# Linear attention on one core: the stores of heads 28 and 29 become one set, shared between GpSimd and SP

## The chip, the core and the metric

The kernel runs on one core of a Trainium2 chip. The metric is device time in microseconds. The time before is the median of three runs, 167.97 us (167.58 to 168.05). The profile is of one more execution, which took 167.82 us; its span, from the first to the last instruction, is 166.5 us. Times inside the kernel are given in us from the start of that span.

A few words for a new reader. TensorE (PE) does matrix products, VectorE (DVE), ScalarE (ACT) and GpSimd (POOL) do elementwise work, and SyncE (SP) issues most of the transfers. A transfer is cut up among 16 DMA engines, and each of them adds one to the transfer's semaphore when its own share has landed.

## The reference: what is computed

Inputs q, k, v are bf16 of shape (1, 32, 2048, 128): 32 heads of 2048 rows of 128. For each head:

```
phi_q = where(q > 0, q + 1, exp(q)) + 1e-6
phi_k = where(k > 0, k + 1, exp(k)) + 1e-6
kv    = phi_k^T v              # 128 x 128
z     = sum over rows of phi_k # 128
out   = (phi_q kv) / (phi_q z + 1e-6)
```

Each head reads 3 x 512 KB and writes 512 KB, so the kernel moves 50.33 MB in and 16.78 MB out.

## The kernel before

**Tiling.** A head's 2048 rows lie on 128 partitions, 16 rows to a partition: partition p holds rows 16p to 16p+15, so a partition's share of a head is 16 x 128 x 2 bytes = 4 KB, in one piece in DRAM and in one piece in SBUF. In what follows "a row" of a store means one partition's share, as in the change's title. `NBI` = 6 input buffers each for k, q and v; `NBO` = 10 output buffers `o_sb`, so head h uses output buffer h % 10: heads 28 and 29 lie in the neighbouring buffers 8 and 9, and heads 30 and 31 in 0 and 1.

**Stages of a head.** ACT takes exp(k) (line 368); GpSimd takes the relu of k (372) and adds part of the two halves of phi_k (390); DVE clips the exponential (382); PE builds kv and z in PSUM (413, 320), and ACT copies them to SBUF (430). PE transposes q (436), ACT and DVE make its two halves (447, 454, 456, 468), PE multiplies them with kv (483, 484). DVE adds 1e-6 to the denominators (506), takes reciprocals (512) and multiplies into `o_sb` (517, 524). For the last two heads ACT does a part of these multiplications (536).

**Order.** A planner holds all operations. Every one has an engine and a number, its key; on each engine the operations are emitted in the order of the keys, and the planner adds the semaphore waits that the data need. Loads and stores are emitted on SP. The store of head h has the key h + 1 + 0.18 h (line 575), which places stores behind the loads of later heads, more so the later the head. Behind the last load, SP's list holds only stores; each waits for the last DVE multiplication of its head. The last operation of GpSimd's list is the memset of ones for head 31 (line 426); after it GpSimd has nothing to do.

**The stores at the end** (lines 570 to 584). A store is issued by `store`, which takes a range of partitions. All heads up to 30 are stored by one transfer of 128 rows, except head 29: `PARTS` cuts it into transfers of 51, 13 and 64 rows, all three on SP and on the semaphore of output buffer 9. Head 31 is stored by two transfers of 128 partitions: nine tiles (288 KB), then seven (224 KB). At the very end SP waits for the semaphores of all output buffers.

Of the kernel before, what the change touches and what calls it, by code (L numbers as in the profile page):

```python
# [7 lines left out]
P = 128  # L8
# [223 lines left out]
def bass_standalone__linear_attn_elu__prompt_kernel(  # L232
# [8 lines left out]
    NT = 16  # L241
# [3 lines left out]
    NBI = 6  # L245
    NBO = 10
# [2 lines left out]
    NG = 7  # L249
    HALF = NT * P // 2  # L250
    LAST = NH - 1
    PARTS = {LAST - 2: (51, 13, 64)}

    ADD = (10, 11, 12, 13, 14)
    EVEN, ODD = tuple(range(0, NT, 2)), tuple(range(1, NT, 2))
# [7 lines left out]
    of = out.rearrange("b h s d -> (b h) s d")  # L263

    with ExitStack() as es:
        def sb(name, shape, dt):
            return es.enter_context(nc.sbuf_tensor(name, shape, dt))
# [13 lines left out]
        o_sb = sb("o_sb", [P, NBO, NT, D], bf16)  # L281
# [12 lines left out]
        def dma_sem(name):  # L294
            return dsems[name]

        for n, c in (("k", NBI), ("q", NBI), ("v", NBI), ("va", 1), ("o", NBO + 1)):
            for i in range(c):
                dsems[(n, i)] = es.enter_context(nc.semaphore(f"s_{n}{i}"))

        pl = Plan()

        def rows(x, h):
            return x[h].rearrange("(p j) d -> p (j d)", j=NT)
# [11 lines left out]
               reads=[("id0",)], writes=[("ident",)])  # L316
# [34 lines left out]
        for h in range(NH):  # L351
# [3 lines left out]
            bi, b2, b3, bo = h % NBI, h % 2, h % 3, h % NBO  # L355

            def load(name, buf, src, key, h=h, bi=bi):
                dst, rws = buf[:, bi], rows(src, h)
                if name == "v":
# [9 lines left out]
                   reads=[("k", bi)], writes=[("ek", b2)])  # L369
# [8 lines left out]
            else:  # L378
# [4 lines left out]
                   reads=[("ek", b2)], writes=[("emk", b3)], kind="emk")  # L383
# [36 lines left out]
            if h:  # L420
                pl.add("pe", at("kv", -1.2), lambda pe, kv=kv, t=both_of: kv(pe, t, start=True),
                       reads=[("emk", b3), ("rk", b3, 0), ("rk", b3, 1)] + base, writes=[("bankkv",)])
            pl.add("pe", at("kv", -1.199), lambda pe, kv=kv, t=one_of, f=h == 0: kv(pe, t, start=f, stop=f),
                   reads=[("phix" if h == 1 else "phik", b3)] + base + ([] if h else [("first",)]), writes=[("bankkv",)])
            if h:
                pl.add("pool", h + 0.6, lambda g, bi=bi: g.memset(_ap(vfull, bi * VW + GAP + D - 1, [[2 * D, NT // 2], [1, 1]]), 1.0),
                       reads=[("v", bi)], writes=[("vo", bi)], kind="vo")
                pl.add("pe", at("kv2", -0.2985), lambda pe, kv=kv: kv(pe, ODD, stop=True),
                       reads=[("phik", b3), ("emk", b3), ("rk", b3, 0), ("rk", b3, 1), ("v", bi), ("vo", bi)], writes=[("bankkv",)])
            pl.add("act", at("kvs", -0.95), lambda a, b3=b3: a.activation(kvs_sb[:, b3, :], kvz_ps[:, 0:NC], ACT.Copy),  # L430
                   reads=[("bankkv",)], writes=[("kvs", b3)], kind="kvs")
# [31 lines left out]
            else:  # L463
# [5 lines left out]
                   reads=[("eq", b2, 0), ("eq", b2, 1)], writes=[("emq", b3)], kind="emq")  # L469
# [100 lines left out]
            def store(t0, t1, key, parts, slot, p0=0, p1=P, h=h, bo=bo):  # L570
                pl.add("sp", key, lambda sp: sp.dma_start(rows(of, h)[p0:p1, t0 * D:t1 * D],
                                                          o_sb[p0:p1, bo, t0:t1].rearrange("p j d -> p (j d)")),
                       reads=[("o", bo, p) for p in parts], dma=("o", slot))

            late = h + 1.0 + 0.18 * h
            if h < LAST:
                p0 = 0
                for n in PARTS.get(h, (P,)):
                    store(0, NT, late, ("t", 0, 1, 2, 3, 4), bo, p0, p0 + n)
                    p0 += n  # L580
                assert p0 == P
            else:
                store(0, 9, late, (0, 1, 2), bo)
                store(9, NT, late + 0.01, (3, 4, "t"), NBO)

# [29 lines left out]
```

## Time and profile before

| what | value |
|---|---|
| median of 3 runs | 167.97 us |
| the profiled execution | 167.82 us |
| its span | 166.5 us |
| PE, DVE, ACT, GpSimd busy | 156.0, 152.3, 155.0, 106.3 us |
| bytes moved, mean rate over the span | 67.25 MB, 404 GB/s |
| last load issued by SP (v of head 31) | 135.79 us |
| GpSimd's last instruction | 156.37 us, 0.13 us long |
| store of head 28 issued | 152.48 us |
| the three stores of head 29 issued | 157.20 to 158.48 us |
| store of head 30 issued | 160.94 us |
| the two stores of head 31 issued | 162.20 and 162.87 us |

How to read it: the busy times are of the whole span, so they say little of the last ten microseconds, in which the engines stop one after the other and only transfers are left. Those are read from the table of windows (busy time of each engine, share of the DMA engines' time in which a packet was under way, and GB/s) and from the semaphore increments that the trace records, one for each DMA engine that has landed its share of a transfer.

### The profile page before, as it was taken

The numbers are of one execution on the slowest core, as the hardware profiler recorded it, in microseconds if no ns is written. First come the engines' busy times: TensorE is split into PE (matmuls) and PEld (weight loads), VectorE is DVE, ScalarE is ACT, GpSimd is POOL, SyncE is SP. The second block draws the span as 40 slices with busy tenths as digits, with TensorE's granted clock in tenths as the row PEclk, the third lists the DMA queues.
The fourth block names the chain that finished last, engine by engine and source line by source line (L and its number), as shares of the span: only waits on it lengthen the run. The fifth ranks groups of instructions, "written<-read, shape, count | busy, mean of one in ns | idle before, by whom it ended". The sixth has DMA issues, their size and how long they took to land.

```text
span 166.5 us, 6269 instructions
## 1 busy us (share of the span) xinstructions
PE 156.0 (94%) x2819; PEld 145.3 (87%) x2453; DVE 152.3 (91%) x270; ACT 155.0 (93%) x143; POOL 106.3 (64%) x128
## 2 busy tenths in 40 slices
PE   7789999999999999999999999999999999999960
PEld 0259999999999999899999989999998999999950
DVE  0587999999999999999999999999999999999991
ACT  3979999999999999999999999999999999998790
POOL 2405788676767877676778867676787767677300
PEclk9999999999999999999999999999999999999998
DMA  5999999999999999999999999999999999999986
GB/s 205 345 417 421 413 415 419 412 407 418 417 416 419 422 417 417 422 421 411 424 420 414 423 421 415 419 421 415 422 420 416 422 421 418 418 421 418 415 310 239
DMA packets 18605, 67.25 MB, mean 404 GB/s; under 512 B 2082, under 2 KB 2210, under 8 KB 18594
## 3 DMA queue, kind: packets, MB, share of 16 engines
q1 hardware_dynamic: 18592, 67.12, 99.4%
q8 instruction: 5, 0.08, 0.2%
q14 instruction: 6, 0.05, 0.1%
q10 hardware_dynamic: 2, 0.00, 0.0%
HBM read 50.33 MB, written 16.78 MB: 403 GB/s over the span
## 4 chain that ended last, share of the span: by engine, by line
DVE 58%; PE 17%; POOL 12%; ACT 6%; issue 3%; DMA 2%; DVEq 0%
DVE o_sb L524 20%; POOL rk_sb L390 12%; DVE rq_sb L456 11%; DVE emk_sb L382 10%; DVE emq_sb L468 9%; PE kvz_ps L413 6%; PE o_ps L483 5%; PE o_ps L484 5%; ACT ek_sb L368 3%; DVE rden_sb L512 3%; DVE o_sb L517 3%; ACT eq_sb L447 2%; DMA k_sb<-in_k_dram 2%; DVE den_sb L506 2%; DVE rk_sb L390 1%
## 5 line engine op out<-in xcount | busy, mean ns | idle before, releaser
L413 PE MATMUL kvz_ps<-v_sb,rk_sb 128*128 128x129 bf16 (+1 forms) x512 | 67.0, 220 | 2.8 <-DVE rk_sb L390 1.0
L524 DVE TENSOR_TENSOR o_sb<-o_ps,rden_sb 128x768 bf16<-128x768 f32 (+2 forms) x62 | 67.8, 1135 | 0.0
L390 POOL TENSOR_TENSOR rk_sb<-rk_sb,emk_sb 128x640 bf16<-128x640 bf16 x30 | 41.9, 1395 | 39.5 <-DVE emq_sb L468 38.2
L372 POOL TENSOR_SCALAR rk_sb<-k_sb 128x1024 bf16<-128x1024 bf16 (+1 forms) x60 | 64.1, 1068 | 2.5 <-DMA k_sb<-in_k_dram 2.5
L483 PE MATMUL o_ps<-kvs_sb,emq_sb 128*128 128x129 bf16 (+1 forms) x536 | 65.2, 217 | 0.0
L484 PE MATMUL o_ps<-kvs_sb,rq_sb 128*128 128x129 bf16 (+1 forms) x536 | 64.4, 217 | 0.0
L368 ACT ACTIVATE ek_sb<-k_sb 128x2048 bf16<-128x2048 bf16 x32 | 61.0, 1907 | 2.6 <-DMA k_sb<-in_k_dram 2.6
L447 ACT ACTIVATE eq_sb<-xT_ps 128x2048 bf16<-128x2048 bf16 (+1 forms) x33 | 60.0, 1821 | 2.0 <-PE xT_ps L436 2.0
L413 PE MATMUL kvz_ps<-v_sb,emk_sb 128*128 128x129 bf16 (+1 forms) x338 | 53.3, 221 | 0.6 <-DVE emk_sb L382 0.3
L413 PEld LDWEIGHTS kvz_ps<-v_sb,rk_sb 128*128 128x128 bf16 x512 | 46.1, 98 | 7.6 <-POOL rk_sb L390 2.7
L483 PEld LDWEIGHTS o_ps<-kvs_sb,emq_sb 128*128 128x128 bf16 x536 | 51.2, 98 | 0.8 <-issue 0.3
L484 PEld LDWEIGHTS o_ps<-kvs_sb,rq_sb 128*128 128x128 bf16 x536 | 51.3, 98 | 0.0
L436 PE MATMUL xT_ps<-ident,q_sb 128*128 128x128 bf16 x512 | 33.8, 219 | 0.6 <-DMA q_sb<-in_q_dram 0.4
L436 PEld LDWEIGHTS xT_ps<-ident,q_sb 128*128 128x128 bf16 x512 | 29.9, 98 | 5.1 <-DMA q_sb<-in_q_dram 4.2
L413 PEld LDWEIGHTS kvz_ps<-v_sb,emk_sb 128*128 128x128 bf16 x338 | 32.5, 98 | 0.9 <-DVE emk_sb L382 0.5
L320 PE MATMUL kvz_ps<-ones_sb,rk_sb 128*128 128x1 bf16 x232 | 31.3, 165 | 0.0
L454 ACT ACTIVATE rq_sb<-xT_ps 128x1024 bf16<-128x1024 bf16 x30 | 30.9, 1029 | 0.0
L382 DVE TENSOR_SCALAR emk_sb<-ek_sb 128x2048 bf16<-128x2048 bf16 x32 | 22.0, 688 | 5.6 <-ACT ek_sb L368 5.6
L456 DVE TENSOR_SCALAR rq_sb<-xT_ps 128x1024 bf16<-128x1024 bf16 x34 | 23.3, 690 | 1.1 <-PE o_ps L484 1.0
L468 DVE TENSOR_SCALAR emq_sb<-eq_sb 128x2048 bf16<-128x2048 bf16 x32 | 22.1, 690 | 0.0
L320 PE MATMUL kvz_ps<-ones_sb,emk_sb 128*128 128x1 bf16 x121 | 19.9, 166 | 0.0
L430 ACT ACTIVATE kvs_sb<-kvz_ps 128x129 bf16<-128x129 f32 x32 | 9.0, 281 | 1.6 <-PE kvz_ps L413 0.9
(28 smaller groups left out, 49.2 us busy)
## 6 DMA issues: line engine op xcount, KB each, us to landing
k_sb<-in_k_dram SPq DMA_DIRECT2D x32, 512.0 KB, 15.0
q_sb<-in_q_dram SPq DMA_DIRECT2D x32, 512.0 KB, 15.1
v_sb<-in_v_dram SPq DMA_DIRECT2D x32, 512.0 KB, 15.1
out_dram<-o_sb SPq DMA_DIRECT2D x30, 512.0 KB, 15.3
out_dram<-o_sb SPq DMA_DIRECT2D x1, 288.0 KB, 3.7
out_dram<-o_sb SPq DMA_DIRECT2D x1, 256.0 KB
out_dram<-o_sb SPq DMA_DIRECT2D x1, 224.0 KB, 3.6
out_dram<-o_sb SPq DMA_DIRECT2D x1, 204.0 KB
```

The costliest lines, as they stand in the source:

```text
L320: return pe.add_instruction(mybir.InstMatmult(start_tensor_calc=start, stop_tensor_calc=stop, ldweights=False, bass_skip_group_check=True, ...
L368: lambda a, bi=bi, b2=b2: a.activation(ek_sb[:, b2, :], k_sb[:, bi, :], ACT.Exp),
L372: pl.add(eng, key, lambda e: e.tensor_scalar(rk_sb[:, b3, c], k_sb[:, bi, c], BIG, 0.0, op0=ALU.min, op1=ALU.max), reads=[("k", bi)] + ([( ...
L382: lambda d, b2=b2, b3=b3: d.tensor_scalar(emk_sb[:, b3, :], ek_sb[:, b2, :], 1.0, EPS, op0=ALU.min, op1=ALU.add),
L390: return e.tensor_tensor(out=a, in0=a, in1=b, op=ALU.add)
L413: last = pe.matmul(kvz_ps[:, 1 - l:NC], lhsT=w, rhs=v_sb[:, bi, c - l:c + D], start=first, stop=fin, skip_group_check=True)
L436: last = pe.transpose(xT_ps[:, j * P:(j + 1) * P], q_sb[:, bi, j * P:(j + 1) * P], ident[:])
L447: halves[part] = pl.add("act", key, lambda a: a.activation(eq_sb[:, b2, c], xT_ps[:, c], ACT.Exp), reads=both[part:part + 1] or both, writ ...
L456: f = lambda d: d.tensor_scalar(rq_sb[:, b3, c], xT_ps[:, c], 0.0, None, op0=ALU.max)
L483: pe.matmul(o_ap, lhsT=emq_sb[:, b3, t * P:(t + 1) * P], rhs=kvs_sb[:, b3, c0:c1], start=True, stop=False)
L484: return pe.matmul(o_ap, lhsT=rq_sb[:, b3, t * P:(t + 1) * P], rhs=kvs_sb[:, b3, c0:c1], start=False, stop=True)
L524: pl.add("dve", key, lambda d: d.tensor_tensor(out=o_sb[:, bo, 3 * g0:3 * g1, :].rearrange("p (a b) d -> p a b d", b=3), in0=_ap(full, bas ...
```

## The change

Heads 28 and 29 are no longer stored one by one. Nothing is issued when head 28 is ready. When head 29 is ready too, eight transfers are issued, each of which takes the same partitions of both heads, so that a row is now 2 x 4 KB: GpSimd issues one of 5 rows (partitions 0 to 4) and one of 99 rows (5 to 103), and SP issues six of 4 rows (104 to 127). The two on GpSimd get semaphores of their own; the six on SP use that of output buffer 9. Their key is that of head 29's store before. Bytes and values are the same, and all other operations stay as they are.

```diff
-    PARTS = {LAST - 2: (51, 13, 64)}
+    TWO = (("pool", NBO + 1, 5), ("pool", NBO + 2, 99)) + (("sp", NBO - 1, 4),) * 6
...
-        for n, c in (("k", NBI), ("q", NBI), ("v", NBI), ("va", 1), ("o", NBO + 1)):
+        for n, c in (("k", NBI), ("q", NBI), ("v", NBI), ("va", 1), ("o", NBO + 3)):
...
             late = h + 1.0 + 0.18 * h
-            if h < LAST:
+            if h == LAST - 2:
                 p0 = 0
-                for n in PARTS.get(h, (P,)):
-                    store(0, NT, late, ("t", 0, 1, 2, 3, 4), bo, p0, p0 + n)
+                for eng, slot, n in TWO:
+                    p = slice(p0, p0 + n)
+                    pl.add(eng, late, lambda e, p=p, bo=bo: e.dma_start(
+                        of[LAST - 3:LAST - 1].rearrange("h (p j) d -> p h (j d)", j=NT)[p], o_sb[p, bo - 1:bo + 1].rearrange("p h j d -> p h (j d)")),
+                        reads=[("o", b, x) for b in (bo - 1, bo) for x in ("t", 0, 1, 2, 3, 4)], dma=("o", slot))
                     p0 += n
                 assert p0 == P
-            else:
+            elif h < LAST and h != LAST - 3:
+                store(0, NT, late, ("t", 0, 1, 2, 3, 4), bo)
+            elif h == LAST:
                 store(0, 9, late, (0, 1, 2), bo)
                 store(9, NT, late + 0.01, (3, 4, "t"), NBO)
```

## The prediction

> **What bounds the kernel now.** I read the page first for the whole run, then the windows of its end, then SP's and GpSimd's lists, then the semaphore increments of the last stores.
>
> The page, whole run:
>
> ```profile
> span 166.5 us, 6269 instructions
> ...
> PE 156.0 (94%) x2819; PEld 145.3 (87%) x2453; DVE 152.3 (91%) x270; ACT 155.0 (93%) x143; POOL 106.3 (64%) x128
> ...
> DMA  5999999999999999999999999999999999999986
> ...
> q1 hardware_dynamic: 18592, 67.12, 99.4%
> ...
> out_dram<-o_sb SPq DMA_DIRECT2D x30, 512.0 KB, 15.3
> ...
> out_dram<-o_sb SPq DMA_DIRECT2D x1, 224.0 KB, 3.6
> ```
>
> PE, DVE and ACT are all over 90% busy, and the DMA engines are full from the second slice to the 38th; a store in the middle lands 15.3 us after its issue, so it stands in a queue. The change touches none of that, only the end. The windows there (busy time of each engine, clock, DMA share, GB/s):
>
> ```profile
> 158.00:160.00 2.00, 1.91 (x37) 1.74 (x35) 1.89 (x6) 1.83 (x8) 0.00 (x0) 1.00 1.01 363
> 160.00:161.00 1.00, 1.00 (x20) 0.90 (x16) 0.93 (x5) 0.93 (x5) 0.00 (x0) 1.00 0.75 258
> 161.00:162.00 1.00, 0.08 (x2) 0.00 (x0) 0.97 (x4) 0.97 (x4) 0.00 (x0) 1.00 0.58 238
> 162.00:163.00 1.00, 0.00 (x0) 0.00 (x0) 0.84 (x3) 0.73 (x3) 0.00 (x0) 1.00 0.99 373
> 163.00:164.00 1.00, 0.00 (x0) 0.00 (x0) 0.00 (x0) 0.00 (x0) 0.00 (x0) 1.00 0.99 387
> 164.00:165.00 1.00, 0.00 (x0) 0.00 (x0) 0.00 (x0) 0.00 (x0) 0.00 (x0) 1.00 0.70 276
> ```
>
> Between 160 and 162 the DMA engines idle for 0.25 + 0.42 us on the mean, before the last two heads are ready; from 164 on some have finished and others not. So the end is a matter of which DMA engine has how much left. SP's list (start, us, count of issues):
>
> ```profile
> 152.48 0.33 SPq L571 DMA_DIRECT2D out_dram<-o_sb  x1
> ...
> 157.20 1.28 SPq L571 DMA_DIRECT2D out_dram<-o_sb  x3
> ...
> 160.94 0.37 SPq L571 DMA_DIRECT2D out_dram<-o_sb  x1
> ...
> 162.87 0.37 SPq L571 DMA_DIRECT2D out_dram<-o_sb  x1
> ```
>
> These are heads 28, 29, 30 and the second part of 31. The increments of their semaphores, one per DMA engine, say the rest. Head 27 (issued 147.73): the first engine lands at 157.81, the eighth at 158.19, the fifteenth at 160.45, the sixteenth at 161.77. Head 28: 159.06, 159.43, 161.69, and 163.08. One engine, the laggard, is 1.3 to 1.4 us behind the fifteenth, and needs 1.39 us for a head's eight rows of 4 KB where the others need 1.25: 0.174 and 0.156 us a row. Head 29's last increment is at 163.96, head 31's last at 166.48, which is the end; ten of the sixteen were done by 164.94. The laggard is 0.88 us from 163.08 to 163.96, five rows by 0.174: one of the 13-row transfer, four of the 64-row one, none of the 51-row one, whose shares have 17 rows. So an end without a laggard could be up to 166.48 - 164.94 = 1.54 us earlier, and each row more for the laggard costs 0.17 us. Two others of the sixteen land within 0.11 us of it at the end, so a gain is partly covered by them.
>
> **The change part by part.**
>
> *How the shares fall.* The 128-row stores leave sixteen increments, and head 29's three leave 3 + 13 + 16 = 32. So a transfer goes to the largest number of engines up to 16 that divides its rows. By that, 5 rows go to five engines, 99 to eleven with nine rows each, 4 to four. A row is now two pieces of 4 KB. For heads 28 and 29 together an engine of the eleven gets 18 pieces, an engine of SP's four gets 12, one of the five 2. Before it was 8 of head 28 and 4, 5 or 22 of head 29; the laggard had 13. No row shows which engines a GpSimd transfer takes.
>
> *Removed:* four issues on SP (0.33 at 152.48, and 1.28 for three). SP waited before each, so that is worth nothing by itself. Head 28's 512 KB come to the queues 4.7 us later (157.20 for 152.48). The first engine runs out of head 27 at 157.81 and the fifteenth at 160.45. Head 30's store shows how soon new work starts: issue 160.94, first landing 163.47, 2.53 us, of which 8 x 0.156 = 1.25 are its rows; 1.28 is the start and the receipt. SP's first rows so start by 158.5. The leading engines idle about 0.7 us there; they idle before the last heads anyway (shares 0.75 and 0.58). Cost: nothing, as long as they have their pieces done by about 162.2, where head 30's start (160.94 + 1.28).
>
> *Added on SP:* six issues. The nearest row is the mean of the three at 157.20, 1.28 / 3 = 0.43; bounds 0.33 and 0.55. The sum is 2.6 us (2.0 to 3.3), to 159.8 (160.5 at most). Queued behind is head 30's store, at 160.94. Hidden; if head 30 were ready earlier, it would cost up to the 2.6 us. The four engines have 12 pieces x 0.156 = 1.9 us, done by about 160.7. But in 160 to 161 the rate was 258 GB/s at a share of 0.75, that is 344 at full share, for 413 to 422 between 150 and 158: the pieces of the part transfers took longer, single ones 300 to 440 ns in place of 159. At 440 the twelve last 5.3 us, to 163.8, and with 2.52 for heads 30 and 31 (163.96 to 166.48) end at 166.3. I take twice 0.156: no cost.
>
> *Added on GpSimd:* two issues behind its last instruction (156.37, 0.13 long); nothing is queued behind them there and no engine waits for GpSimd any more. The wait is for DVE's last multiplication of head 29, 157.17. Its cost is not in this trace. From below: SP's 0.33 each, pieces at 157.2 + 0.66 + 1.28 = 159.1. From above: GpSimd's longest row, 1.40, each, and 0.69 for one DVE operation in its way, 157.2 + 2.8 + 0.69 + 1.28 = 162.0. I take the middle, 160.5. Eighteen pieces are 2.81 us. On the fifteenth engine, free at 160.45, they end at 163.3 (164.8 by the upper bound), and with 2.52 at 165.8 (167.3).
>
> *The laggard* is not free until 161.77, so GpSimd's start costs it nothing. With 18 pieces, 3.13 us, it is done at 164.90 for 163.96 before: later by 0.94. At the others' rate it would be 2.81 and +0.62. Heads 30 and 31 follow on it as before.
>
> *The sum* for a laggard among the eleven: span 166.48 + 0.94 = 167.4, and with the 1.3 us around the span 168.8. That is against the profiled execution's 167.82, which is 0.15 below the median of 167.97; I leave the 0.15 to the range.
>
> [...]
>
> [...]
>
> **The rivals.**
>
> *A. The laggard is spared (faster).* It is none of the first three engines (five rows, above). If GpSimd's eleven leave it out, it has 2 pieces or none: done by 162.1, before head 30 starts. The fifteenth decides: 165.8, with 0.2 to 0.5 for slower pieces 166.0 to 166.3, and the time is 167.1 to 167.6; I say 167.3. For it: everything that ends after 164.94 is queueing. Against: eleven of sixteen hold any given engine with 0.69. It decides at thirteen pieces: below that the end moves earlier.
>
> *B. A middling share.* Fourteen pieces for the laggard (in SP's four with one of the five, or 99 rows cut into shares of seven): 161.77 + 14 x 0.174 = 164.21, later by 0.25, time 168.1; sixteen give 168.4.
>
> *C. GpSimd is late.* Non-laggards may start their 18 pieces until 163.96 - 2.81 = 161.15 without being later than the laggard was before, 3.95 us after the release at 157.20. Each us beyond costs one. At the upper bound, 162.0, the time is 168.7; at twice that issue cost, 165.5, some 172. For it: GpSimd has issued no transfer before in this kernel, a first one may be dear. Against: it is idle then.
>
> **How the numbers follow.** The laggard among the eleven 0.42, A 0.30 (5 of 16 is 0.31), B 0.13, C 0.15. About 0.3% (0.5 us) is what a measurement of this kernel can tell from no change: 167.5 to 168.5. A gives faster 0.27 and same 0.03; B same 0.08 and slower 0.05; the forecast same 0.02 and slower 0.40; C same 0.01 and slower 0.14. Together 0.27, 0.14, 0.59. The likeliest case alone spans 168.4 (rate 0.156) to 169.3 (0.5 more for slow pieces). The range goes down to A's 166.9 (the fifteenth undisturbed, and 0.2 less) and up to 169.9, where about half of C is left out.
>
> **What would show it.** Right: head 29's semaphores end at about 164.9 or later and one engine alone ends the kernel; head 30's issue stays near 160.9; the set leaves 5 + 11 + 24 increments, or sixteen per GpSimd transfer. A would show as all engines landing within about 1 us at the end. C would show as GpSimd's issues lasting over 1.4 us and a DMA share far below 1 between 158 and 161. The forecast is wrong if the laggard has few pieces, or if it is not slower in this execution.

## The result, and the profile after

The changed kernel takes 169.34 us (median of 10 runs, 168.14 to 170.35), the kernel before 167.91 us on the same chip (10 runs, 167.55 to 168.08). The ratio is 1.0084, 95% interval 1.0063 to 1.0105: it is slower by 0.8%. The sign and the range of the prediction held (168.8 us, 166.9 to 169.9). The reason that it gave did not. The profiled execution took 169.12 us. A few executions of the same kernel ran over 1.5% slower than its fastest; the ratios in this document leave them out, the medians and ranges do not.

The page of the changed kernel: the span, the DMA line of the forty slices, the two data queues (packets, MB, share of 16 engines) and the stores of the end (KB each, us from issue to landing).

```profile
span 167.8 us, 6274 instructions
...
DMA  5999999999999999999999999999999999999894
...
q1 hardware_dynamic: 18360, 66.27, 97.5%
q0 software_dynamic: 352, 0.85, 1.6%
...
out_dram<-o_sb POOLq DMA_DIRECT2D x1, 792.0 KB, 7.4
...
out_dram<-o_sb SPq DMA_DIRECT2D x1, 224.0 KB, 4.6
```

The span is 1.3 us longer than the 166.5 of before. Nothing before the last three slices has changed. GpSimd's 99 rows (792 KB) need 7.4 us from issue to landing, and the last store of the kernel, which was not touched, needs 4.6 in place of 3.6: it is held up by what stands ahead of it on some engine.

The end of the changed kernel by windows (busy time of PE, PEld, DVE, ACT, POOL; clock; DMA share; GB/s):

```profile
157.00:158.00 1.00, 1.00 (x22) 1.00 (x19) 0.93 (x5) 0.71 (x2) 0.94 (x2) 1.00 0.97 361
158.00:159.00 1.00, 0.91 (x17) 0.74 (x15) 0.96 (x3) 0.99 (x4) 0.72 (x1) 1.00 0.50 184
159.00:160.00 1.00, 1.00 (x23) 1.00 (x21) 0.96 (x4) 1.00 (x5) 0.00 (x0) 1.00 0.79 262
160.00:161.00 1.00, 0.65 (x12) 0.47 (x9) 0.93 (x6) 0.93 (x4) 0.00 (x0) 1.00 0.98 279
161.00:162.00 1.00, 0.00 (x0) 0.00 (x0) 0.97 (x6) 0.97 (x5) 0.00 (x0) 1.00 0.96 312
162.00:163.00 1.00, 0.00 (x0) 0.00 (x0) 0.41 (x1) 0.30 (x2) 0.00 (x0) 0.91 1.00 295
163.00:164.00 1.00, 0.00 (x0) 0.00 (x0) 0.00 (x0) 0.00 (x0) 0.00 (x0) 0.50 0.97 370
164.00:165.00 1.00, 0.00 (x0) 0.00 (x0) 0.00 (x0) 0.00 (x0) 0.00 (x0) 0.50 0.90 338
165.00:166.00 1.00, 0.00 (x0) 0.00 (x0) 0.00 (x0) 0.00 (x0) 0.00 (x0) 0.50 0.62 241
```

Read the last two columns together. From 158 to 160 the share is 0.50 and 0.79, where it was 1.01 before: head 28 is no longer there to fill it. From 160 to 163 the share is 0.96 to 1.00, so the engines are busy, but they move only 279 to 312 GB/s; at such a share the middle of the run moves 418. The pieces take longer. That is 1 - 295/418, some 30% of the engines' time, for three microseconds.

SP's and GpSimd's lists of issues (start, us, count), from the two timelines:

```profile
156.77 2.74 SPq L580 DMA_DIRECT2D out_dram<-o_sb  x6
160.51 3.71 SPq L571 DMA_DIRECT2D out_dram<-o_sb  x3
```

```profile
157.05 1.67 POOL L580 DMA_DIRECT2D out_dram<-o_sb  x2 [0.98 <-DVE o_sb L524]
```

SP's six issues cost 0.46 us each and are over at 159.51, GpSimd's two 0.74 and 0.93. The increments and the packets of the trace say the rest. GpSimd's first piece starts at 158.94. SP's 24 rows land between 158.95 and 163.81. Of the eleven engines that carry the 99 rows, ten land between 163.20 and 164.20 and one at 165.25. One engine alone ends the kernel: of the last store, fifteen increments come by 166.72 and the sixteenth at 167.79, 1.07 us later.

That is the picture which the prediction gave for its likeliest case, with one engine ending alone, 165.25 for 164.90 and a span of 167.8 for 167.4. It is a coincidence, as the first experiment showed. The loss is also larger than the spans say, since this execution issued the set earlier: from SP's first issue of the set to the end of the span are 9.3 us before (157.20 to 166.5) and 11.1 here (156.77 to 167.8), 1.8 us more.

### The profile page after: what moved, and what is told of

The parts are those of the page before. It is cut to its first block, busy times and chain, and to the rows that moved or that the text cites. A ratio compares the mean times of both kernels' runs of the same rounds, so it can differ in the third digit from the quotient of the medians.

```text
span 167.8 us, 6274 instructions
## 1 busy us (share of the span) xinstructions
PE 156.1 (93%) x2819; PEld 145.5 (87%) x2453; DVE 152.1 (91%) x270; ACT 154.9 (92%) x143; POOL 107.9 (64%) x130
## 3 DMA queue, kind: packets, MB, share of 16 engines
q1 hardware_dynamic: 18360, 66.27, 97.5%
## 4 chain that ended last, share of the span: by engine, by line
DVE 58%; PE 17%; POOL 12%; ACT 6%; issue 2%; DMA 2%; DVEq 0%
DVE o_sb L524 20%; POOL rk_sb L390 12%; DVE rq_sb L456 11%; DVE emk_sb L382 9%; DVE emq_sb L468 9%; PE kvz_ps L413 6%; PE o_ps L483 5%; PE o_ps L484 5%; ACT ek_sb L368 3%; DVE rden_sb L512 3%; DVE o_sb L517 3%; ACT eq_sb L447 2%; DMA k_sb<-in_k_dram 2%; DVE den_sb L506 2%; DVE rk_sb L390 1%
```

## The experiments

The theory to start with was the prediction's: the laggard, the engine that lands head 27's store 1.3 us behind the fifteenth in the profile of before and 1.8 us behind it here (161.75 for 159.96), is among GpSimd's eleven and has 18 pieces. The rivals were that the laggard is spared and another engine ends last, that GpSimd's issue is late, and that the pieces are slow. From the seventh experiment on the question was where a spared laggard's gain went.

### Which engine is the laggard

The changed kernel with thirteen small loads, of 3 to 15 rows of 64 bytes, on SP behind head 27's store. A load of n rows goes to n engines: the 117 rows of the thirteen loads add 234 packets to SP's queue (18594 for the change's 18360), one increment for each row. If they are taken from the same end each time, the first length whose last increment is late names the laggard. The loads are extra work.

```diff
...
+        for i in range(13):
+            n = i + 3
+            pl.add("sp", 32.9 + 0.01 * i, lambda sp, n=n, i=i: sp.dma_start(tag_sb[0:n, i, :], qf[0, 0:n, 0:32]),
+                   writes=[("tag", i)], dma=("t", i))
```

> The changed kernel with thirteen tiny loads added on SP behind head 27's store, of 3, 4, ... 15 rows of 64 bytes, each on a semaphore of its own; SP is idle there (147.6 to 156.8 us) and they move 7 KB. They only count: a load of n rows goes to n engines, so the smallest n whose last increment comes with the laggard (1.8 us behind the next engine in the changed kernel's profile) gives the laggard's place among the engines, if part transfers always take the engines from the same end. Laggard theory: one n from which on every last increment is about 1.8 us later than below it; place 4 to 13, from its five rows of head 29 before. If the place is 5 to 13, no row of SP's six transfers is on it. Rival (no fixed laggard, or the engines are taken in turn): last increments that jump to and fro with n. Time as the changed kernel's, about 169.3.

Measured: 169.37 us. The last increment of the load of 3 rows comes at 159.01, of 4 rows at 160.28, of 5 rows at 163.11, and of all longer ones at 163.30 to 165.05. The late engine also runs eleven of the small reads in one burst from 162.12, as an engine must that is in the loads of 5 to 15 rows. So the laggard is the fifth engine, counted from the end from which such transfers take them.

What follows: the 5-row transfer takes five engines and the 99-row one the other eleven, if GpSimd starts at the first. Then the fifth has 2 pieces and is spared. In the changed kernel's trace the two increments of such an engine can be found: head 27 at 161.75, the 5 rows at 162.13, two pieces of 0.159 us later, and the 99 rows, of which it has none, at 162.33. The same three steps are in the kernel with strided transfers further down: 162.24, 162.53, 162.72. The theory's main step has fallen, and the cause of the loss was open again.

### The 99 rows ahead of the 5

```diff
-    TWO = (("pool", NBO + 1, 5), ("pool", NBO + 2, 99)) + (("sp", NBO - 1, 4),) * 6
+    TWO = (("pool", NBO + 1, 99), ("pool", NBO + 2, 5)) + (("sp", NBO - 1, 4),) * 6
```

> The changed kernel with GpSimd's two transfers in the other order: 99 rows first (partitions 0 to 98), then 5 (99 to 103). If the engines of a GpSimd transfer are taken in turn, 5 first and 11 next, the order changes who gets 18 pieces and who 2: a laggard among the last five goes from 18 pieces to 2 and the time falls to about 167.5; one among the first five goes from 2 to 18 and the time rises by up to 2.8 us, to 172; one in the middle keeps 18 and the time stays at 169.3. If a GpSimd transfer always starts at the same engine with equal shares, the pieces of an engine are the same in either order and the time stays at 169.3 whoever the laggard is. Rival that blames GpSimd's late start: the big transfer now starts about 0.7 us earlier (the first issue lasted 0.74), so up to 0.7 faster, 168.6.

Measured: 170.52 us (4 runs), ratio to the kernel before 1.015 (1.0091 to 1.0209), for the change's 1.0084 (1.0063 to 1.0105): slower by the medians, with intervals that still overlap. The windows of this run near the end:

```profile
163.00:164.00 1.00, 0.00 (x0) 0.00 (x0) 0.99 (x3) 0.88 (x3) 0.00 (x0) 1.00 0.55 205
164.00:165.00 1.00, 0.00 (x0) 0.00 (x0) 0.00 (x0) 0.00 (x0) 0.00 (x0) 1.00 0.35 123
165.00:166.00 1.00, 0.00 (x0) 0.00 (x0) 0.00 (x0) 0.00 (x0) 0.00 (x0) 1.00 0.65 258
```

A share of 0.35 is 5.6 engines of 16. If GpSimd starts at the first engine, the 99 rows now fall on engines 1 to 11: the laggard has 18 pieces, and SP's four have 18 + 12 = 30. Most engines stand idle at 164 while a few work. Read so, the order of two transfers without a data dependence decides which engines carry them.

That GpSimd's two transfers take the engines in turn, from the first on, was the author's assumption and is not shown by itself. The count (two pieces on the fifth engine) and the swap (a share of 0.35 at 164) agree with it.

### One transfer for both heads, by SP or by GpSimd

Two runs that keep the late release of head 28 and take away the cut into parts. All engines get 8 rows of both heads, 16 pieces.

```diff
-    TWO = (("pool", NBO + 1, 5), ("pool", NBO + 2, 99)) + (("sp", NBO - 1, 4),) * 6
+    TWO = (("sp", NBO - 1, 128),)
```

> Heads 28 and 29 in one SP transfer of 128 rows of both heads, in place of the eight: the late release of head 28 stays, GpSimd and the 4-row transfers go, and every engine has 16 pieces. Laggard theory: it has 16 pieces where before it had 13, so 3 x 0.174 = 0.5 more than before: 168.4. If GpSimd's late start or the slow 4-row transfers are the whole loss, no part of it is left: 167.9, as before. If the late release of head 28 itself is the loss (engines idle between head 27 and the set), 169 or more.

```diff
-    TWO = (("pool", NBO + 1, 5), ("pool", NBO + 2, 99)) + (("sp", NBO - 1, 4),) * 6
+    TWO = (("pool", NBO + 1, 128),)
```

> The same single transfer of 128 rows of both heads, issued by GpSimd. It differs from the one on SP by GpSimd's issue alone. Laggard theory: the same as on SP, 168.4, as the laggard is busy until 161.75 in either case. Rival, GpSimd's start binds: its first pieces came 1.9 us after the release in the changed kernel's profile (157.05 to 158.94), SP's first about 1.1 after, so 0.8 us later than the one on SP, 169.2, and a DMA share below 0.6 around 158 to 159.

Measured: by SP 168.21 us (10 runs), ratio 1.0024 (0.9999 to 1.0050); by GpSimd 168.38 us (10 runs), ratio 1.0039 (1.0017 to 1.0061). The same second of the two, by SP and then by GpSimd:

```profile
158.00:159.00 1.00, 1.00 (x18) 0.83 (x15) 0.97 (x3) 0.80 (x4) 0.00 (x0) 1.00 0.99 393
```

```profile
158.00:159.00 1.00, 1.00 (x20) 0.92 (x17) 0.96 (x3) 0.72 (x3) 0.50 (x1) 1.00 0.37 147
```

GpSimd's start leaves the engines idle for 0.6 us at 158 (share 0.37 for 0.99), yet the time is only 0.17 us longer. With no parts at all, both heads late and the laggard loaded with 16 pieces, the kernel is still about 1 us faster than the change. So neither the late release nor GpSimd's issue holds most of the loss. What is left is in the parts.

### The parts by themselves

Both heads stored by one SP transfer of 128 rows, and the three kinds of transfer of the change repeated after all has landed: the six, the 5 rows and the 99 rows one after the other, and then the 99 rows and the six together. `again` issues such a transfer; `ends` are the last stores of the kernel, and each step waits for the one before it. The repeats are extra work, so this kernel's time of 190.19 us says nothing.

```diff
...
+        for i in range(6):
+            x = again("sp", 50 + 0.01 * i, 0, 104 + 4 * i, 4, ends if i == 0 else [])
+        x = again("pool", 51, 1, 0, 5, [x])
+        x = again("pool", 52, 2, 5, 99, [x])
+        y = again("pool", 53, 3, 5, 99, [x])
+        for i in range(6):
+            again("sp", 53 + 0.01 * i, 4, 104 + 4 * i, 4, [x] if i == 0 else [])
```

> A measurement, not a version: heads 28 and 29 in one SP transfer, and behind the last store, when all has landed, the changed kernel's transfers once more with the same rows and bytes, each by itself: SP's six of 4 rows, then GpSimd's 5 rows, then its 99, and at last the 99 and the six together. Shares of the 99: if eleven engines have nine rows each, they land at one time, about 18 x 0.156 = 2.8 us after the first piece, and five have no piece; if sixteen have shares of seven, fourteen land after 2.2 us. The six: with free reading 12 x 0.156 = 1.9 us from the first piece to the last; if four engines reading neighbouring partitions share one way in, the first transfer alone takes 1.2 us and the six 3 us or more, up to 7.5 us, with pieces of 300 to 640 ns. GpSimd's start by itself: 1.9 us from issue to first piece as in the changed kernel, or less if DVE was in its way there. Time 12 us or more above the others, of no meaning.

The windows of this run while only the six transfers of 4 rows are under way, and then while only the 99 rows are:

```profile
168.00:169.00 1.00, 0.00 (x0) 0.00 (x0) 0.00 (x0) 0.00 (x0) 0.00 (x0) 0.50 0.18 45
169.00:170.00 1.00, 0.00 (x0) 0.00 (x0) 0.00 (x0) 0.00 (x0) 0.00 (x0) 0.50 0.24 57
170.00:171.00 1.00, 0.00 (x0) 0.00 (x0) 0.00 (x0) 0.00 (x0) 0.00 (x0) 0.50 0.19 74
...
178.00:179.00 1.00, 0.00 (x0) 0.00 (x0) 0.00 (x0) 0.00 (x0) 0.00 (x0) 0.50 0.68 250
```

Four engines of 16 are a share of 0.25. At 0.24 they move 57 GB/s, 15 GB/s an engine, and in the third second 74 at 0.19, 24 an engine; the eleven of the 99 rows move 250 at 0.68, 23 GB/s an engine. Of the six's 48 pieces, 4 KB each, the first seven take 352 to 664 ns, with nothing else on the queues; a free one takes 159, as most of the later ones do, and the mean of all is 252. The 5 rows' ten pieces look the same: eight take 284 to 619 ns and two, of one engine, 160 and 156, as if four neighbouring rows slowed each other and the fifth stood apart. The 99 rows' pieces take 188 ns on the mean. The six need 3.6 us from the first piece to the end of the last, for issues that are themselves spread over 2.6 us. The 99 rows leave five increments within 0.8 us of the first piece and eleven at 179.98 to 180.40: five engines carry none of it, eleven carry nine rows. GpSimd's first pieces start 1.32 and 1.36 us after the issue. The six and the 99 together need 8.4 us, for 4.7 and 5.4 alone; but which engines carried the 99 that second time, and whether SP's four were among them, is not shown, so that last number can't be carried over to the change.

### Which engine ends alone

The changed kernel with seven small loads, of 4 to 14 rows, behind the last store. They are extra work.

```diff
...
+        for i, n in enumerate((4, 5, 6, 8, 10, 12, 14)):
+            pl.add("sp", 40.0 + 0.01 * i, lambda sp, n=n, i=i: sp.dma_start(tag_sb[0:n, i, :], qf[0, 0:n, 0:32]),
+                   writes=[("tag", i)], dma=("t", i))
```

> The changed kernel with seven tiny loads on SP behind its last store, of 4, 5, 6, 8, 10, 12 and 14 rows of 64 bytes: each engine reaches its own only when its queue is empty, so they tell which engine ends last. Laggard theory: the load of 5 rows and all longer ones land last, with the kernel's last store, the load of 4 rows earlier. Rival, SP's four engines end last (12 pieces of their own that are read slowly): the load of 4 rows lands last already. Rival, one of the eleven with 18 pieces: the loads of 4 and 5 land early, a longer one late. The loads add up to about 1 us to the time by themselves.

Measured: 170.49 us. The kernel's own last increment comes at 168.68, the one before it at 167.35. The loads of 4, 5, 6, 8 and 10 rows have landed by 167.78, the one of 12 by 168.22, 1.37 us after its issue and so undelayed. The engine that ends alone is none of the first twelve: not SP's four, not the laggard, but one of the last four, which by the order of engines assumed above have 18 of GpSimd's pieces.

### The six as one transfer of 24 rows

```diff
-    TWO = (("pool", NBO + 1, 5), ("pool", NBO + 2, 99)) + (("sp", NBO - 1, 4),) * 6
+    TWO = (("pool", NBO + 1, 5), ("pool", NBO + 2, 99), ("sp", NBO - 1, 24))
```

> SP's six transfers of 4 rows become one of 24 rows, which goes to twelve engines with two rows each; GpSimd's two stay. If the slow reading of the six is the loss, the time falls to 168.2, as with one SP transfer for all (168.21). If the 18 pieces on eleven engines are, it stays or rises: those among the first twelve now have 22, 169.3 to 169.9. Laggard theory: if it has 2 pieces of the five rows and 14 or none of the 99, it now has 4 in place of 0 from SP, 0.7 us later: 170.0 if it ends last.

Measured: 168.51 us (10 runs), ratio 1.0013 (0.9987 to 1.0040). The 24 rows go to twelve engines, two rows each (SP's queue has 18348 packets for the change's 18360, 12 increments in place of 24), and land by 162.55 where the six landed by 163.81. Most of the change's loss is gone. This run alters several things, the number of engines, the number of issues and what each transfer reads, so the next one keeps the six issues and their engines.

### The six over partitions that lie apart

The same six transfers of 4 rows, to the same four engines, 12 pieces for each. Only the rows differ: every sixth partition in place of four neighbours, and with it every sixth row in DRAM.

```diff
-                    p = slice(p0, p0 + n)
+                    p = slice(p0, p0 + n) if eng == "pool" else slice(104 + (p0 - 104) // 4, P, 6)
```

> The changed kernel with one thing different: each of SP's six transfers takes four partitions that lie six apart (104, 110, 116, 122 and so on) in place of four neighbours. Shares, engines, queues and bytes are the same. If neighbours read one at a time are the loss, SP's pieces go back to 159 ns, its rows land by about 161 in place of 163.8, and the time falls to 168.2. If the loss is the 18 pieces or the laggard, the time stays at 169.3.

Measured: 168.38 us (10 runs), ratio 1.0016 (0.9988 to 1.0045), for the change's 1.0084 (1.0063 to 1.0105). The two intervals don't meet. The end of this kernel by windows:

```profile
160.00:161.00 1.00, 1.00 (x24) 1.00 (x21) 0.96 (x2) 1.00 (x5) 0.00 (x0) 1.00 0.68 193
161.00:162.00 1.00, 0.73 (x13) 0.55 (x10) 0.93 (x5) 0.93 (x5) 0.00 (x0) 1.00 0.90 287
162.00:163.00 1.00, 0.00 (x0) 0.00 (x0) 0.96 (x6) 0.97 (x4) 0.00 (x0) 1.00 0.92 307
163.00:164.00 1.00, 0.00 (x0) 0.00 (x0) 0.50 (x2) 0.39 (x2) 0.00 (x0) 1.00 0.99 344
164.00:165.00 1.00, 0.00 (x0) 0.00 (x0) 0.00 (x0) 0.00 (x0) 0.00 (x0) 1.00 1.00 396
```

The heads of this execution are ready about 1 us later than in the change's profile (GpSimd issues at 158.14, for 157.05), and the span is still 0.3 us shorter: from SP's first issue of the set to the end are 9.7 us (157.85 to 167.5), for 11.1 in the change. No engine ends alone: fifteen increments by 167.12, the last at 167.47. So most of the loss, about 1 us, lies in the choice of neighbouring rows for each of SP's transfers. Whether it is that they are neighbours in SBUF or in DRAM this run does not separate. The strided issues are dearer, 0.69 us each, and hold head 30's store until 162.1, which is to the disadvantage of the stride; that they are spaced more widely could also help it, and was not tried by itself.

One thing expected of this run did not come. SP's rows land no sooner: by 164.92, 7.1 us after its first issue, for 7.0 in the change. Nor are GpSimd's pieces faster on the mean, 204 ns for 205. What differs is where the slow ones fall. On SP's queue, from the set's first pieces to 6.5 us after its first issue, head 30's included, 23 pieces take over 250 ns in the change, up to 787, and 16 with the stride, up to 460. And the eleven engines of the 99 rows land 6.1 to 6.7 us after SP's first issue with the stride, for 6.4 to 7.4 and one at 8.5 in the change.

The isolated transfers agree in direction: with neighbouring rows the four engines moved 45 to 74 GB/s in the windows above, and the first seven pieces took 352 to 664 ns for 159 of a free one. One of the six quite alone no run shows. What neighbouring rows have in common that slows them, and which rows an engine has, is not shown either; that it also slows engines with GpSimd's rows, since an engine behind the twelfth was late, remains the author's guess.

### The late release alone

The kernel before, with head 28's store put beside head 29's three.

```diff
-                p0 = 0
-                for n in PARTS.get(h, (P,)):
-                    store(0, NT, late, ("t", 0, 1, 2, 3, 4), bo, p0, p0 + n)
-                    p0 += n
-                assert p0 == P
+                for g in (() if h == LAST - 3 else (h - 1, h) if h == LAST - 2 else (h,)):
+                    p0 = 0
+                    for n in PARTS.get(g, (P,)):
+                        pl.add("sp", late, lambda sp, g=g, p=slice(p0, p0 + n): sp.dma_start(
+                            rows(of, g)[p], o_sb[p, g % NBO].rearrange("p j d -> p (j d)")),
+                            reads=[("o", x % NBO, y) for x in {g, h} for y in ("t", 0, 1, 2, 3, 4)], dma=("o", g % NBO))
+                        p0 += n
+                    assert p0 == P
```

> The kernel before with one thing moved: head 28's store, still one transfer of 128 rows on SP, waits for head 29 and is issued right ahead of head 29's three. Shares and rows are those of before. If the late release is part of the loss, the DMA engines idle around 158 to 159 and the time rises by up to the difference that one transfer for both heads showed (168.21 for 168.01), 168.2 to 168.4; if that difference came from the laggard's three pieces more, the time stays at 168.0.

Measured: 168.72 us (12 runs, 168.12 to 171.37), for 168.11 of the kernel before on that chip (29 runs); ratio 1.0018 (0.9996 to 1.0040). The late release costs up to 0.4% and can't be told from nothing here. Its profiled execution took 169.92 us, so it is read for nothing else.

### Head 29 alone by GpSimd, with the laggard spared

If the laggard's share sets the end, then keeping head 28 as it was and sparing the laggard in head 29 should gain. Two variants of the kernel before: 5 + 121 rows by GpSimd and 2 by SP, then 5 + 99 and six strided ones. The transfers are issued from these lists where `PARTS` was.

```diff
-    PARTS = {LAST - 2: (51, 13, 64)}
+    ONE = (("pool", NBO + 1, slice(0, 5)), ("pool", NBO + 2, slice(5, 126)), ("sp", NBO - 1, slice(126, P)))
...
```

> A version: head 28's store as before, at its own time on SP. Head 29 alone is shared: 5 rows by GpSimd (first five engines), 121 by GpSimd (eleven rows of 4 KB on each of the other eleven), 2 by SP. The fifth engine, the laggard, has 8 + 1 = 9 pieces for heads 28 and 29, for 13 before: done 4 x 0.174 = 0.7 us earlier. The eleven have 19: the latest of them, free of head 28 at 161.69, is done at 163.4 and with 2.52 at 165.9, which would be the end, 0.5 earlier than 166.48: time 167.4 to 167.5. If pieces read slowly on the eleven cost more than that, 168.0 or above. If the laggard does not set the end of the kernel before, no change.

```diff
-    PARTS = {LAST - 2: (51, 13, 64)}
+    ONE = (("pool", NBO + 1, slice(0, 5)), ("pool", NBO + 2, slice(5, 104))) + tuple(("sp", NBO - 1, slice(104 + i, P, 6)) for i in range(6))
...
```

> As the version with 121 rows, but with the change's shares for head 29 alone: 5 and 99 rows by GpSimd, six transfers of 4 rows lying six partitions apart by SP. The laggard has 9 pieces, the eleven 17, the first four 15. By shares the end is 0.3 us earlier than with 121 rows, 167.2; but SP's six issues took 0.62 each with such rows, 3.7 us together from 157.2 to 160.9, when head 30 is ready, so head 30's store may be up to 0.3 us late: 167.2 to 167.5. If slow reading by rows out of order is the greater cost, 168 or more.

Both missed: 168.51 us, ratio 1.0018 (1.0001 to 1.0035), and 168.48 us, ratio 1.0023 (0.9999 to 1.0046), 12 runs each. The lines of GpSimd's queue (packets, MB, share), the variant with 121 rows first and then the one with 99:

```profile
q0 software_dynamic: 176, 0.52, 1.0%
```

```profile
q0 software_dynamic: 160, 0.43, 0.8%
```

They tell why. The first has 126 pieces of 4 KB, 32 increments, and 18 packets of 4 bytes more. In these runs an engine without data gets one such packet for each piece that the others have. The 5 rows leave 11, one on each of eleven engines. Eleven shares of eleven rows would leave 5 x 11 = 55 for the 121 rows; there are 7. Sixteen shares of 8, the last cut to 1, leave 7. Likewise 160 - 104 - 32 = 24, less 11, is 13 for the 99 rows: sixteen shares of 7, of which one is cut to 1 and one empty, leave 6 + 7 = 13. Eleven shares of nine would leave 45. In the change, where a row is two pieces, 352 - 208 - 32 = 112 = 11 x 2 + 5 x 18: there it is eleven shares of nine.

So the laggard was not spared. It has 8 rows of head 28 and 9 of head 29 in the first variant, 8 and 8 in the second, for 13 of both before. Head 30's last increment follows from head 27's at 0.159 us a row: 161.87 + (17 + 8) x 0.159 = 165.85, measured 165.84; 161.77 + (16 + 8) x 0.159 = 165.59, measured 165.59. The laggard's share does set its own end, and in the first variant the kernel's: fifteen engines are done at 165.30, the sixteenth at 167.07.

So these two runs show sixteen shares of equal rounding-up for rows of one piece (7 and 13 small packets), and the change shows eleven equal shares for rows of two (5 x 18).

### Halves, so that the laggard is spared

A version that follows from this. SP stores tiles 0 to 7 of heads 28 and 29, 128 rows each, when each head is ready. The other halves of both go together, with rows of two pieces, as 5 + 99 rows by GpSimd and six strided transfers by SP. The laggard has 4 + 4 + 1 = 9 rows' worth. `TWO` now holds the row ranges 0 to 4, 5 to 103 and the six strided ones.

```diff
...
+                half = h in (LAST - 3, LAST - 2)
+                store(0, NT // 2 if half else NT, late, ("t", 0, 1, 2, 3, 4), bo)
+                if h == LAST - 2:
+                    for eng, slot, p in TWO:
+                        pl.add(eng, late, lambda e, p=p, bo=bo: e.dma_start(
+                            of[LAST - 3:LAST - 1].rearrange("h (p j) d -> p h (j d)", j=NT)[p, :, HALF:],
+                            o_sb[p, bo - 1:bo + 1, NT // 2:].rearrange("p h j d -> p h (j d)")),
+                            reads=[("o", b, x) for b in (bo - 1, bo) for x in ("t", 0, 1, 2, 3, 4)], dma=("o", slot))
```

> Heads 28 and 29 are each stored by SP up to their eighth tile (128 rows of 2 KB) when they are ready; the other halves of both heads go together by GpSimd (5 and 99 rows, two pieces of 2 KB a row) and by six strided transfers of 4 rows on SP. The laggard then has 4 + 4 rows' worth of the two halves and one of the set, 9 where the kernel before gives it 13 and the two one-head variants 16 and 17. Theory that the laggard's share sets the end wherever it is the largest, at 0.159 us a row: the lone late engine of the one-head variants is gone, the shares are 17 rows' worth on eleven engines and 15 on four, and the span is 165.9 to 166.2, the time 167.3 to 167.7, below the kernel before. Packets of 4 bytes on GpSimd's queue: 144, as for the change, since each row is two pieces. Rival, that something else is as late (GpSimd's transfers starting 1.4 us after their issue, or shares of sixteen for these rows too): 168.1 to 168.6, and 80 packets of 4 bytes if the shares are of sixteen.

Measured: 167.62 us (12 runs, 167.24 to 168.51), for 168.47 of the kernel before on that chip (17 runs, 167.65 to 170.65); ratio 0.9957 (0.9933 to 0.9980). It is faster than the kernel before by 0.4%; the change was not run beside it. The page, the windows and SP's list of this run:

```profile
span 166.2 us, 6276 instructions
...
q0 software_dynamic: 192, 0.43, 0.8%
...
out_dram<-o_sb POOLq DMA_DIRECT2D x1, 396.0 KB, 5.0
...
out_dram<-o_sb SPq DMA_DIRECT2D x1, 224.0 KB, 3.0
```

```profile
158.00:159.00 1.00, 1.00 (x22) 1.00 (x20) 0.93 (x5) 0.70 (x4) 1.00 (x2) 1.00 1.00 393
...
161.00:162.00 1.00, 0.37 (x7) 0.19 (x4) 0.93 (x5) 0.93 (x4) 0.00 (x0) 1.00 0.90 318
162.00:163.00 1.00, 0.00 (x0) 0.00 (x0) 1.00 (x4) 0.97 (x4) 0.00 (x0) 1.00 0.32 111
163.00:164.00 1.00, 0.00 (x0) 0.00 (x0) 0.13 (x1) 0.02 (x1) 0.00 (x0) 1.00 1.00 406
```

```profile
157.87 4.13 SPq L581 DMA_DIRECT2D out_dram<-o_sb  x6
162.11 1.68 SPq L571 DMA_DIRECT2D out_dram<-o_sb  x3
```

The share at 158 is 1.00 again, since half of head 28 is there in time. All sixteen increments of the first transfer behind the set, head 30's, come within 0.27 us (164.61 to 164.88), and the last store's within 0.20 (166.00 to 166.20): no engine ends alone, and the last store takes 3.0 us in place of 3.6 before and 4.6 in the change. What limits it now is seen at 162: the engines are idle two thirds of the time, while SP, busy with the six strided issues until 162.00, comes to head 30's store at 162.11 only. Cheaper issues there were not tried. The packet count was not the one expected: 192 - 104 - 32 = 56 small packets, 11 for the 5 rows and 45 = 5 x 9 for the 99, since here the two halves of a row count as one packet of 4 KB; the eleven shares of nine were as expected.

## Why the prediction was right in its time and wrong in its reason

**How the shares fall**: right. Five, eleven with nine rows, and four, by the increments of the isolated transfers and the 112 small packets. It holds for these transfers, not as a rule: 99 rows of one piece left the 13 small packets of sixteen shares, not the 45 of eleven.

**The laggard**: this step failed. It put the laggard among GpSimd's eleven with 18 pieces. It is the fifth engine and has 2, as rival A had it. The prediction weighed the case by the count of engines, 5 of 16, because no row said which engine the laggard was. Rival B, a middling share, is out by the same count. With the laggard spared, rival A's 167.1 to 167.6 would have followed if all else had been as costed. The rate of the step was off too: at the end the laggard takes 0.159 us a row, not 0.174.

**Added on SP**: this step failed too. "No cost" was worked out with pieces of 0.156 us, done by 160.7, and held when they were taken twice as slow. In the change they landed by 163.81, about the step's upper bound (163.8), and single pieces took up to 787 ns. By the step's own sum even that bound ends SP's four engines at 166.3 and costs nothing, and with the stride SP's rows land as late. So the price is not the lateness of SP's four, which is all that the step priced. It falls on the others: the engine that ends last is one of the last four, with GpSimd's rows. Spreading the same rows took the ratio from 1.0084 to 1.0016.

**Added on GpSimd**: right in its verdict, and nearer the cheap side. The first piece started at 158.94, 2.2 us after SP's first issue, with issues of 0.74 and 0.93 us; the step's bounds are 1.9 and 4.8 us after the release, and it took 3.3. No run shows the term of 0.69 us in the upper bound, a DVE operation in GpSimd's way: the first piece came 1.89 us after GpSimd's first issue in the change (157.05 to 158.94), with DVE 0.93 and 0.96 busy from 157 to 159, and 1.32 and 1.36 us after it in the isolated transfers, with all engines still; what makes the difference is not shown. Exchanging SP for GpSimd in the whole transfer cost 0.17 us. Rival C is out.

**Removed**: roughly right. The late release leaves the share at 0.50 and 0.79 where it was 1.01, and by itself costs between nothing and 0.4%. It is not free as a matter of course: the version that keeps half of head 28 early has a share of 1.00 there.

**The sum**: 167.4 for the span, measured 167.8; counted from the first issue of the set, 0.94 us more than before was forecast and 1.8 measured. The 0.94 us that it charged to the laggard are not the laggard's; what took their place came with SP's six transfers of neighbouring rows. Two errors, a laggard that was spared and transfers that were priced at nothing, nearly cancelled, and that the time fell into the range is luck. The sign of a laggard with more pieces was sound all the same: with 16 and 17 rows its end is met to 0.01 us at 0.159 us a row, and the version that leaves it 9 is 0.4% faster than the kernel before.

**Still open**: why in the change one particular engine of the last four ends 1.07 us after the rest. Its last four pieces of the 99 rows, from 163.48 on, took 291, 291, 418 and 388 ns, together 0.75 us more than free ones; then it ran head 30's eight at 159 ns each, from 164.91 on. SP's part transfers, landed by 163.81, were through by then. What ran slow beside those four were pieces of head 30 on another engine, 262 to 293 ns each. So that part of its delay arose beside head 30, and how SP's six transfers lead to it, no run shows. It doesn't happen with strided rows. What the rows' being neighbours has to do with it is not shown.

## What to carry to other kernels

When the end of a kernel is a matter of which DMA engine has how much left, find out which engine the late one is before shifting work between engines; a handful of small loads of 3, 4, 5 ... rows does it in one run. When a transfer is cut into parts for a few engines, try parts whose rows lie apart, and compare share with rate: a share of 1.00 at 295 GB/s in place of 418 means slow pieces. And a way of splitting has to be read off the trace for the very shape that is used, since the same 99 rows went to eleven engines with two pieces a row and to fifteen with one.

## What the runs showed of the hardware that was not expected

- Four 4 KB rows from neighbouring partitions, read by four engines at one time with nothing else under way, took 352 to 664 ns a piece at the start of SP's six transfers and 284 to 619 in GpSimd's 5 rows, for 159 ns free. Later in the six, most pieces took 159.
- GpSimd cut 99 rows of one piece into sixteen shares of up to seven (13 small packets; fifteen engines have data) and 99 rows of two pieces into eleven shares of nine (5 x 18 small packets). The engines without data still ran one packet for each missing piece, in the change 112 of 4 bytes, about 6 ns apart.
- An issue on GpSimd takes 0.74 to 0.93 us in the change, with the first piece 1.3 us after its start when all is quiet and 1.9 us in the change. An issue on SP of four rows with a stride takes 0.69 us, for 0.46 with neighbours in the change.
- The laggard falls behind while the stores run back to back: in the kernel before it lands a head every 1.32 to 1.40 us over heads 21 to 28, where the fifteenth increment comes every 1.22 to 1.27, and its lag grows from 0.3 us (152.05 for 151.73) to 1.4 (163.08 for 161.69). At the end, with other engines idle, it takes 0.159 us a row over 24 and 25 rows, about a free piece for each. Why it is slower under load was not looked into.
